# A never-taken, hinted branch at the end of TensorE's and VectorE's programs

## The chip, the cores, the metric

The kernel runs on one core of a Trainium2 chip. The metric is the device time of one execution in microseconds. A profiled execution also has a *span*, from its first to its last instruction. The time is a little longer than the span; below, time minus span of the same execution is called the **excess**. Spans of single runs are kept to 0.1 us, so a single excess is known to about 0.05 us. In the kernel before, the excess was 1.21 to 1.39 us in every run for which both are known. The engines go by the profiler's names: PE is TensorE, DVE is VectorE, ACT is ScalarE, POOL is GpSimd, and SP (SyncE) issues the output store and all loads but x's 2 KB, which ACT issues.

## The reference

One decode step: x plus grouped-query attention over a cache of 65,536 keys (4 KV heads, 32 query heads, head size 128), plus a small two-layer MLP branch, all in bf16.

```python
xn = _layernorm(x)
# A: q = xn @ wq; softmax(q k^T / sqrt(128)) v per head; @ wo
# B: x1 = xn + shift-mixed gelu(ln(xn) @ w1) @ w2;  x1 + gelu(ln(x1) @ w3) @ w4
return x + _A_ref(xn, k_cache, v_cache, wq, wo) + _B_ref(xn, w1, w2, w3, w4)
```

With one token there is almost no arithmetic per byte. The kernel's work is to read 170 MB of cache and weights once.

## The kernel before

The program records each engine's operations in a list (`q_pe`, `q_dve`, `q_act`, `q_pool`, `q_sp`), with semaphore waits worked out from the buffers, and then emits the lists one engine after another. All loads but x's go through SP's DMA queue; K and V arrive in 8 MB blocks, and the next block is issued when its slot is free. The main part, cut:

```python
for m in range(NBLK):                 # 8 blocks of 32768 keys, two per KV head
    ...
    Ttr(n); QK(n); ...                # DVE transposes K, PE multiplies
    MAX(..); EXP(..); PT(..); PV(..)  # softmax and P @ V
    issue(6 + 2 * m)                  # next loads
    ...
    if nb == BPH - 1:
        combine(h)
...
resid_rows()
wo_rows()
for i, (r0, nr) in enumerate(w4_parts):      # w4 comes in four pieces: 17, 7, 3, 1 rows
    out_rows([...], [b_W4[i], b_gh], last=...)
_op(q_dve, lambda e: e.tensor_copy(orow[:, :], OUT), ...)
ev_out = _dma(q_sp, chan("out"), lambda e: e.dma_start(out=..., in_=orow[0:97:32, :]), ...)
q_sp.wait_all([ev_out])                      # SP alone waits for the output
```

DVE's program is one straight line of about 270 instructions. PE's has a loop over the four heads, and after it the straight tail:

```python
q_dve.emit(nc.vector)
...
with nc.tensor.Fori(0, HKV):
    ...
q_pe.emit(nc.tensor, q_pe.ops[marks[-1]:])   # everything after the loop
```

## Time and profile before

| | before |
|---|---|
| median time of the first three runs | 400.42 us (400.32 to 400.59) |
| span of the profiled run | 399.1 us |
| bytes read | 169.87 MB, 426 GB/s over the span |
| instruction packets after the first instruction | five of 16,384 bytes, two of 8,192 bytes |

From the page of the kernel before: the line of the span; the rows of DMA share (each digit is a fortieth of the span, 9 means 90% or more) and GB/s; the DMA queues with packets, MB and the share of the 16 DMA engines' time; and the shares of the chain of waits.

```profile
span 399.1 us, 3429 instructions
...
DMA  9999899999999999999999999999999999999995
GB/s 420 420 388 493 383 441 466 447 415 427 420 427 429 434 460 434 434 427 420 434 427 420 466 440 434 421 420 434 427 427 466 434 440 420 420 427 434 418 414 229
...
q1 hardware_dynamic: 3608, 169.87, 98.7%
q8 instruction: 5, 0.08, 0.1%
q10 hardware_dynamic: 144, 0.00, 0.0%
q14 instruction: 2, 0.02, 0.0%
HBM read 169.87 MB, written 0.00 MB: 426 GB/s over the span
...
DMA 59%; DVE 25%; PE 12%; issue 1%; ACT 1%; SPq 1%; POOL 0%
```

DMA holds 59% of the chain that ended last. The two `instruction` queues, q8 and q14, bring program code. They take 0.1% of the engines' time, which seems too little to matter. The page counts two packets on q14 after the first instruction.

From the chain of waits of the kernel before, its end (start us, length us, what):

```profile
363.64 32.91 DMA KV<-in_B_w_dram
396.56 0.04 issue
396.60 0.31 PE S_ps L566 x4
396.91 0.02 issue
396.94 0.42 DVE orow L647
```

The last piece of w4 lands at 396.56 us; four matmuls and a copy follow. From the timeline, the output store:

```profile
397.39 0.63 SPq L648 DMA_DIRECT2D out_dram<-orow  x1
```

Its wait ends at 399.08 us, and with it the span. Now the same queues in two stretches: 255 to 262 us, and 392 to 396 us, where the last pieces of w4 arrive (DMA view restricted to a window).

```profile
DMA packets 59, 3.02 MB, mean 432 GB/s; under 512 B 12, under 2 KB 12, under 8 KB 12
...
q1 hardware_dynamic: 58, 3.01, 100.2%
q14 instruction: 1, 0.01, 0.3%
```

```profile
q1 hardware_dynamic: 283, 1.06, 65.7%
q8 instruction: 1, 0.02, 1.7%
```

Each stretch has one instruction packet among the data packets. The packet records give the times of all seven (start us from the span's start, length us, bytes):

```
q8   46.00  1.09  16384      q14   52.71  0.33  8192
q8   81.76  1.03  16384      q14  259.38  0.33  8192
q8  122.72  1.02  16384
q8  378.24  1.07  16384
q8  394.28  1.08  16384
```

The first two q8 packets fall 257 PE instructions apart (182 and 439 had started before them); the third comes 268 later, and the last two, both behind the loop, are 301 apart. Before the two q14 packets 51 and 190 DVE instructions had started.

```
241.76 .79 .82 .87 .88 .92 .98 242.03 .11 .27 .38 .39 | 242.90 243.35 243.53 243.71
261.12 .15 .18 .23 .24 .28 .35 .39 .47 .64 .75 .75   | 262.71 262.89 263.07 263.24
394.45 .48 .52 .56 .61 .66 .81 .88 .96 395.07 .08    | 396.02 396.11 396.20 396.39 396.56
```

Twelve engines form a pack. Four are late by 0.51, 0.96, 1.14 and 1.32 us after the pack's last one in the first row. In the second row, after the packet at 259.38 us, the engine with 0.51 is gone and one with 1.49 is there. In the last row the pack has lost one more engine, after the q8 packet at 378.24 us. The same comparison around q8's first three packets shows one engine of the pack 1.55 to 1.56 us later each time, so a 16 KB packet cost more than the "about 1 us" that the prediction below gives every fetch.

### The profile page before, as it was taken

What the parts mean: (1) busy time and instruction counts of PE and PEld (TensorE: products, weight loads), DVE (VectorE), ACT (ScalarE), POOL (GpSimd) and SP (SyncE); (2) the same over time, 40 slices, a digit from 0 to 9 for tenths busy, and PEclk for the clock granted to TensorE, in tenths of its full rate; (3) what the DMA queues carried; (4) which work ended last, traced back from release to release, by engine and by line L of the source; (5) the groups of instructions that cost most, each with busy time, mean ns of one, the idle gap of its engine ahead of it and who ended that gap; (6) DMA issues with size and microseconds to landing.
All of it is one profiled execution on the core that took longest, in us unless ns stands there. A gap on an engine that the chain in (4) does not pass through costs nothing.

```text
span 399.1 us, 3429 instructions
## 1 busy us (share of the span) xinstructions
PE 168.9 (42%) x1523; PEld 59.0 (15%) x1484; DVE 221.4 (55%) x260; ACT 23.9 (6%) x50; POOL 7.7 (2%) x31
## 2 busy tenths in 40 slices
PE   0034767338033713460357036413541362137394
PEld 0011334012001210110012001101120110012232
DVE  0024222994298549833984597269647952895201
ACT  1000000011001100110011002000100110011000
POOL 5000000000000000000000000000000000000000
PEclk9998568555655665575557555855585558555969
DMA  9999899999999999999999999999999999999995
GB/s 420 420 388 493 383 441 466 447 415 427 420 427 429 434 460 434 434 427 420 434 427 420 466 440 434 421 420 434 427 427 466 434 440 420 420 427 434 418 414 229
DMA packets 3759, 169.97 MB, mean 426 GB/s; under 512 B 548, under 2 KB 552, under 8 KB 808
## 3 DMA queue, kind: packets, MB, share of 16 engines
q1 hardware_dynamic: 3608, 169.87, 98.7%
q8 instruction: 5, 0.08, 0.1%
q10 hardware_dynamic: 144, 0.00, 0.0%
q14 instruction: 2, 0.02, 0.0%
HBM read 169.87 MB, written 0.00 MB: 426 GB/s over the span
## 4 chain that ended last, share of the span: by engine, by line
DMA 59%; DVE 25%; PE 12%; issue 1%; ACT 1%; SPq 1%; POOL 0%
DMA KV<-in_A_k_cache_dram 45%; DVE KV L460 18%; DMA KV<-in_B_w_dram 8%; DMA KV<-in_A_x_dram 6%; PE S_ps L411 3%; PE OT_ps L518 2%; DVE mrow L481 2%; PE M_ps L426 2%; PE S_ps L474 2%; PE S_ps L379 1%; ACT p_sb L496 1%; DVE Yall L395 1%; DVE pT_f L509 1%; DVE pT_f L419 1%; PE PT_ps L505 0%
## 5 line engine op out<-in xcount | busy, mean ns | idle before, releaser
L460 DVE STREAM_TRANSPOSE KV<-KV 128x4096 f32<-128x4096 f32 x32 | 140.3, 4422 | 44.3 <-DMA KV<-in_A_k_cache_dram 44.3
L474 PE MATMUL S_ps<-KV,Ycur 128*32 128x512 bf16 x512 | 60.7, 624 | 132.5 <-DVE KV L460 132.5
L518 PE MATMUL OT_ps<-KV,pT_f 128*32 128x512 bf16 x512 | 47.2, 511 | 4.0 <-issue 3.0
L474 PEld LDWEIGHTS S_ps<-KV,Ycur 128*32 128x32 bf16 x512 | 14.3, 126 | 160.0 <-DVE KV L460 142.4
L496 ACT ACTIVATE p_sb<-S_ps,brun 128x1024 bf16<-128x1024 f32 x16 | 17.8, 1114 | 276.6 <-DVE brun L494 176.1
L509 DVE STREAM_TRANSPOSE pT_f<-PT_ps 128x512 f32<-128x512 f32 x32 | 22.5, 702 | 14.0 <-PE PT_ps L505 14.0
L481 DVE TENSOR_REDUCE mrow<-S_ps 128x1 f32<-128x1024 f32 x16 | 19.3, 1205 | 11.3 <-PE S_ps L474 11.3
L484 PE MATMUL M_ps<-Rm,Lmat 128*128 128x16 bf16 x16 | 3.1, 194 | 38.0 <-DVE Rm L482 38.0
L529 DVE SCALAR_TENSOR_TENSOR O_acc<-O_acc,ff,OT_ps 128x512 f32<-128x512 f32 x12 | 9.0, 748 | 14.7 <-PE OT_ps L518 14.7
L518 PEld LDWEIGHTS OT_ps<-KV,pT_f 128*32 128x32 bf16 x512 | 13.1, 115 | 23.8 <-issue 16.4
L411 PE MATMUL S_ps<-KV 128*32 128x512 bf16 x88 | 12.1, 538 | 2.7 <-DVE KV L359 2.7
L339 DVE CAST KV<-KV 128x8 f32<-128x8 bf16 x1 | 0.2, 172 | 22.2 <-DMA KV<-in_A_x_dram 22.2
L578 PE MATMUL S_ps<-KV,o_bf 128*1 128x512 bf16 x64 | 9.9, 484 | 4.5 <-DMA KV<-in_A_wo_dram 4.5
L505 PE MATMUL PT_ps<-p_sb,permR 128*128 128x512 bf16 x16 | 9.7, 607 | 0.8
L426 PE MATMUL M_ps<-ident_f,pT_f 64*128 64x2 f32 (+2 forms) x32 | 7.9, 373 | 2.5 <-DVE pT_f L419 2.5
L484 PEld LDWEIGHTS M_ps<-Rm,Lmat 128*128 128x128 bf16 x16 | 1.7, 104 | 49.3 <-DVE Rm L482 49.3
L582 DVE COPY pT_f<-S_ps 1x512 f32<-1x512 f32 x1 | 0.7, 679 | 14.4 <-PE S_ps L578 14.4
L426 PEld LDWEIGHTS M_ps<-ident_f,pT_f 64*128 64x128 f32 (+2 forms) x32 | 7.7, 326 | 4.7 <-DVE pT_f L419 3.1
L419 DVE COPY pT_f<-S_ps 64x512 f32<-64x512 f32 (+1 forms) x3 | 2.1, 685 | 10.8 <-PE S_ps L411 10.8
L505 PEld LDWEIGHTS PT_ps<-p_sb,permR 128*128 128x128 bf16 x32 | 3.3, 102 | 27.5 <-ACT p_sb L496 14.7
L364 PE MATMUL M_ps<-KV 8*128 8x8 bf16 x1 | 0.2, 184 | 16.1 <-DVE Dmat_f L363 16.1
L642 POOL MEMSET pT_f<- 64x512 f32 x1 | 0.5, 520 | 312.4 <-PE OT_ps L518 312.4
(88 smaller groups left out, 90.2 us busy)
## 6 DMA issues: line engine op xcount, KB each, us to landing
KV<-in_B_w_dram SPq DMA_DIRECT2D x1, 7168.0 KB, 48.0
KV<-in_B_w_dram SPq DMA_DIRECT2D x1, 4352.0 KB, 27.4
KV<-in_B_w_dram SPq DMA_DIRECT2D x2, 2048.0 KB, 28.3
KV<-in_B_w_dram SPq DMA_DIRECT2D x1, 1792.0 KB, 31.3
KV<-in_B_w_dram SPq DMA_DIRECT2D x1, 768.0 KB, 32.7
KV<-in_B_w_dram SPq DMA_DIRECT2D x1, 256.0 KB, 32.9
KV<-in_A_k_cache_dram SPq DMA_DIRECT2D x8, 46.7
KV<-in_A_v_cache_dram SPq DMA_DIRECT2D x8, 28.1
```

The source lines that it names most:

```text
L411: fns.append(lambda e, j=j, k=k, mv=mv: e.matmul(S_ps[32 * (k % 4):32 * (k % 4) + 32, bank + k // 4, :], vec[:, j:j + 1].broadcast_to([P, ...
L419: _op(q_dve, lambda e, b=b, nb=nb: e.tensor_copy(pT_f[0:32 * nb, b, :], S_ps[0:32 * nb, bank + b, :]), reads=[b_S[bank + b]], writes=[b_pT ...
L426: fns.append(lambda e, b=b, nb=nb, c=c: e.matmul(M_ps[:, c0 + 16 * b + c:c0 + 16 * b + 4 * nb:4], pT_f[0:32 * nb, b, c:512:4], ident_f[0:3 ...
L460: _op(q_dve, lambda e: e.transpose(out=KV32[:, s, o:o + 4096], in_=KV32[:, s, o:o + 4096]), reads=[b_KV[s][sub]], writes=[b_KV[s][sub]], l ...
L474: fns.append(lambda e, we=we, cm=cm, mv=mv: e.matmul(S_ps[32 * cm:32 * cm + 32, n % 4, :], Ycur[:, we, :, :].rearrange("p a g -> p (a g)") ...
L481: _op(q_dve, lambda e: e.reduce_max(mrow[:, k:k + 1], S_ps[:, 2 * k:2 * k + 2, :].rearrange("p b c -> p (b c)"), axis=AX.X), reads=b_S[2 * ...
L496: _op(q_act, lambda e: e.activation(p_sb[:, :, :].rearrange("p b c -> p (b c)"), S_ps[:, 2 * k:2 * k + 2, :].rearrange("p b c -> p (b c)") ...
L505: _op(q_pe, lambda e: e.matmul(PT_ps[:, :], permR[:, :], p_sb[:, n % 2, :], start=True, stop=True), reads=[b_p[n % 2], b_const], writes=[b ...
L509: _op(q_dve, lambda e: e.transpose(out=pT_f[:, n % 2, :], in_=PT_ps[:, :]), reads=[b_PT], writes=[b_pT[n % 2]], loop=True)
L518: fns.append(lambda e, q=q, q4=q4: e.matmul(OT_ps[32 * q4:32 * q4 + 32, g % 2, :], pT_bf[:, n % 2, q, :, 1], KV[:, s, 8192 * sub + 512 * q ...
L529: _op(q_dve, lambda e: e.scalar_tensor_tensor(out=O_acc[:, 0:512], in0=O_acc[:, 0:512], scalar=ff[:, k:k + 1], in1=OT_ps[:, k, :], op0=ALU ...
L578: _grp(q_pe, [lambda e, j=j, jj=jj: e.matmul(S_ps[32 * jj:32 * jj + 1, 1, :], o_bf[:, j:j + 1], KV[:, 0, j * D + 512 * jj:j * D + 512 * (j ...
```

## The change

The intent: an instruction packet for code that never runs in the kernel costs DMA time for nothing. So the last block of code on PE and DVE starts with a branch hint (the trace lists it as BRANCH_PREFETCH_HINT, in the profiled run of the change at 142.49 us on DVE and 391.07 us on PE, 0.05 us each) and ends with the branch that the hint is tied to in the program, which is never taken. The intent is to keep away the packets that come last; whether a hint does that is for the runs to show.

```diff
             if nb == BPH - 1:
                 combine(h)
+            if m == 1:
+                dve_cut = len(q_dve.ops)
 ...
         wo_rows()
+        pe_cut = len(q_pe.ops)
 ...
-        q_dve.emit(nc.vector)
+        def hinted_tail(eng, ops, at, name):
+            q, e = ops, eng.engine
+            never = eng.alloc_register(name + "_r")
+            eng.reg_mov(never, 1)
+            nc.br(name + "_b", engines=[e])
+            label(name + "_t")
+            eng.nop(nofuse=True)
+            nc.br(name + "_end", engines=[e])
+            label(name + "_b")
+            hint = eng.mark_branch_hint_location()
+            q.emit(eng, q.ops[at:])
+            eng.wait_ge(ev_out[0], ev_out[1])
+            eng.br_eq(never, 0, on_true=name + "_t", on_false=name + "_end").branch_hint(hint)
+            label(name + "_end")
+        q_dve.emit(nc.vector, q_dve.ops[:dve_cut])
+        hinted_tail(nc.vector, q_dve, dve_cut, "dve")
 ...
-        q_pe.emit(nc.tensor, q_pe.ops[marks[-1]:])
+        q_pe.emit(nc.tensor, q_pe.ops[marks[-1]:pe_cut])
+        hinted_tail(nc.tensor, q_pe, pe_cut, "pe")
 ...
```

One line is cut here: the code is now in several blocks, and the pass that drops repeated weight loads is pointed at the right one; the count of weight loads stays 1484. PE and DVE now wait for the output before they leave, which only SP did before.

## The prediction

> **What bounds the kernel.** The DMA stream does. The page's slice rows show DMA at 9 tenths or more in 39 of 40 slices at about 427 GB/s; 169.87 MB are read in 399.1 us. The chain of waits gives DMA 59% of the span, DVE 25%. DVE is 55% busy, PE 42%. The last load (the last row of w4) lands at 396.56 us, and only 2.5 us follow it.

> **What the change touches.** Instruction fetches. [...] the DMA part of the page lists two instruction queues, and the packet records put five 16,384-byte packets on q8 (at 46.0, 81.8, 122.7, 378.2 and 394.3 us; 1.02 to 1.09 us each[...]) and two packets of 8,192 bytes, half that size, on q14 (52.7 and 259.4 us; 0.33 us each), which I read as DVE's. The last of each, 394.3 and 259.4 us, should be the useless ones[...].

> **What they cost.** The 16 completion increments of each load show the 16 DMA engines one by one. Before the first fetch they lie within 0.6 us; from then on each fetch puts one engine about 1 us behind for good[...]. The 259.4 us fetch moves one engine from 0.52 to 1.5 us behind the pack. That engine becomes the last to land, but only 0.17 to 0.18 us after the next laggard, which other fetches, that stay, have made late. So without it the last load should land at about 396.39 instead of 396.56 us: 0.17 us gained. The 394.3 us fetch came when its engine was nearly done with the last load: between the last two w4 pieces all sixteen increments moved by 0.64 to 0.65 us except two, by 0.72 and 0.74, both early ones. Its removal gains nothing.

> **What it adds.** PE and DVE each get a register move, two branches, a nop (jumped over), a hint, a wait on the output and the closing compare-branch. The trace has 29 ns for a move and 76 ns for an untaken compare-branch (207 to 226 taken). The front part runs while both engines wait for DMA, so it costs nothing. The closing branch runs after the output landed: about 0.1 us at the end, which takes back half of the gain.

> **Prediction.** 400.3 us, range 399.9 to 400.7; faster by over 2%: 0.5%, within 2%: 98.5%, slower: 1%.

> **What would show each step right or wrong.** q14 should have one packet inside the kernel instead of two, q8 four instead of five. The landings after 260 us should have four laggards at most 1.32 us behind the pack, until the 378 us fetch adds a fifth. The last w4 landing moves by 0.1 to 0.25 us. Last instructions should be PE's or DVE's branch, not SP's wait.

> **What would make it wrong.** [...] A block not prefetched may have to be fetched on demand when the engines run on past the kernel's end, after the output[...]. [...]

The forecast's sum: 0.17 us gained in the span, half of it taken back by about 0.1 us at the end, from 400.42 us, gives the 400.3 us. That the last packet of each queue is useless stands as the author's estimate. The runs bear it out: e4 did without both and gave correct results. "About 1 us" for each fetch is rough: by the increments above it was 0.98 us at 8 KB and 1.55 to 1.56 us at 16 KB, and at the packet of 394.28 us no increment moved against the others by more than 0.1 us.

## The result

| | before | after |
|---|---|---|
| median of six runs | 400.50 us (400.32 to 400.77) | 400.87 us (400.58 to 401.81) |
| span of the profiled run | 399.1 us | 398.8 us |
| last load landed, profiled run | 396.56 us | 396.23 us |
| excess | 1.23 us in the profiled run | 1.48 to 2.71 us, mean 2.02 |

The ratio of the runs is 1.0013, 95% interval 1.0000 to 1.0026. A ratio here is the mean time of one kernel's runs over that of the other's of the same rounds, so it is not quite the ratio of the medians. The median went up while the span of the profiled run went down, and the median lies 0.17 us above the range of the prediction.

The same lines of the page after:

```profile
span 398.8 us, 3437 instructions
...
DMA  9999999999999999999999999999999999999995
...
q1 hardware_dynamic: 3608, 169.87, 98.8%
q8 instruction: 4, 0.07, 0.1%
q10 hardware_dynamic: 144, 0.00, 0.0%
q14 instruction: 2, 0.02, 0.0%
...
DMA 59%; DVE 25%; PE 13%; issue 1%; ACT 1%; SPq 1%; POOL 0%
```

q8 has lost one packet, as predicted. q14 still counts two, which was not. The end of the chain and the output store:

```profile
363.30 32.93 DMA KV<-in_B_w_dram
396.23 0.04 issue
396.28 0.31 PE S_ps L566 x4
396.58 0.02 issue
396.61 0.42 DVE orow L650
```

```profile
397.06 0.63 SPq L651 DMA_DIRECT2D out_dram<-orow  x1
```

Everything from the last landing to the store is as before, only 0.33 us earlier. The front part cost nothing, as predicted, although only DVE was waiting for DMA: DVE ran it from 142.2 to 142.5 us and then stood idle until 146.76 us for a K load; PE ran it from 390.7 to 391.1 us among its matmuls, whose groups L584 and L566 start 0.54 us apart as before (390.73 and 391.27 us, before 390.83 and 391.37). The last instruction is now PE's closing branch, as predicted: SP's wait ends at 398.74 us, 0.34 us earlier than before, and the branch, 0.08 us long, ends the span at 398.82 us. In the stretch of 255 to 262 us:

```profile
DMA packets 61, 3.15 MB, mean 449 GB/s; under 512 B 13, under 2 KB 13, under 8 KB 13
...
q1 hardware_dynamic: 61, 3.15, 103.9%
```

The packet is gone. In 392 to 396 us:

```profile
q1 hardware_dynamic: 290, 1.08, 67.1%
q14 instruction: 1, 0.01, 0.5%
```

PE's packet is gone, but an 8 KB packet on q14 (at 394.00 us by the records) has come in. The increments of the three loads after the change:

```
241.77 .79 .85 .91 .93 .94 .96 .97 242.31 .35 .46 .49 | 243.01 243.51 243.51 243.53
261.13 .16 .23 .26 .30 .30 .32 .35 .68 .70 .82 .85   | 262.37 262.88 262.88 262.89
394.49 .50 .61 .63 .65 .66 395.01 .04 .15 .18 .31    | 395.68 396.18 396.19 396.22 396.23
```

The step between the first two rows is gone: the late engines are 0.52, 1.02 to 1.03 (two) and 1.04 us behind in both. So DVE's packet is gone with its delay, as predicted. What is left to explain is the excess.

### The profile page after: what moved, and what is told of

It is laid out like the page before. It is cut to its first block, busy times and chain, and to the rows that moved or that the text cites. A ratio compares the mean times of both kernels' runs of the same rounds, so it can differ in the third digit from the quotient of the medians.

```text
span 398.8 us, 3437 instructions
## 1 busy us (share of the span) xinstructions
PE 170.4 (43%) x1523; PEld 59.5 (15%) x1484; DVE 221.4 (56%) x260; ACT 23.9 (6%) x50; POOL 7.6 (2%) x31
## 3 DMA queue, kind: packets, MB, share of 16 engines
q1 hardware_dynamic: 3608, 169.87, 98.8%
HBM read 169.87 MB, written 0.00 MB: 426 GB/s over the span
## 4 chain that ended last, share of the span: by engine, by line
DMA 59%; DVE 25%; PE 13%; issue 1%; ACT 1%; SPq 1%; POOL 0%
DMA KV<-in_A_k_cache_dram 45%; DVE KV L460 18%; DMA KV<-in_B_w_dram 8%; DMA KV<-in_A_x_dram 6%; PE S_ps L411 3%; PE OT_ps L518 2%; DVE mrow L481 2%; PE M_ps L426 2%; PE S_ps L474 2%; PE S_ps L379 1%; ACT p_sb L496 1%; DVE Yall L395 1%; DVE pT_f L509 1%; DVE pT_f L419 1%; PE PT_ps L505 0%
```

## The experiments

Two theories were stated first. **A**: what the hint keeps out of the kernel is fetched when the engine runs on past the kernel's code, after the output has landed: outside the span, inside the time. **B**: the closing waits and branches themselves make the end longer. The kernels of one group ran on one chip, beside runs of the kernel before. Judged by time alone, most of them cannot be told from the kernel before: only the intervals of e8 to e10, e12 and e14 exclude a ratio of 1. So the excess and the traces carry the argument; in the kernel before the excess stays within 0.18 us.

### First group: parts of the change (e1 to e4)

**e1**, the hinted tail on DVE alone (`q_pe.emit(nc.tensor, q_pe.ops[marks[-1]:])` as before):

> Hinted tail on DVE alone. Theory A (a fetch that the hint keeps out of the kernel is made on demand after the output has landed, outside the span but inside the time): the 8 KB fetch near 259 us is gone and the q8 fetch near 394 us is back; last landing near 396.2 to 396.4, span 398.7 to 399.1. If DVE's own code block runs out after the kernel, the time stays 1.5 us or more above the span and the median is 400.6 to 401; if only PE pays, the excess is back at 1.25 us and the median 400.1 to 400.3. Theory B (the closing waits and branches themselves delay the end): about half of the change's excess, 0.2 us above the kernel before whatever was fetched.

**e2**, on PE alone (`q_dve.emit(nc.vector)` as before):

> Hinted tail on PE alone. Theory A: the q8 fetch near 394 us is gone, the q14 fetch near 259 us is back, last landing 396.5 as before, span 399.1 to 399.2; the time is 400.5 if PE has room left in its last block for what runs after the kernel, and 400.8 to 402 if PE pays on demand. Theory B: about 0.2 us above the kernel before.

**e3**, both tails without the hint:

```diff
-            hint = eng.mark_branch_hint_location()
-            eng.br_eq(...).branch_hint(hint)
+            eng.br_eq(...)
```

> Both tails with their jumps, waits and closing branches, but without the two hint instructions. Theory A: both fetches are back (q14 near 259, q8 near 394), last landing near 396.5, span 399.1 to 399.2, excess of time over span 1.25 us, median 400.5 to 400.6, tight. Theory B: fetches are back too, but the time stays near 400.9 or more with a spread of over 1 us, since waits and branches are all there.

**e4**, the change without the wait for the output:

```diff
-            eng.wait_ge(ev_out[0], ev_out[1])
```

> As the change, but PE and DVE do not wait for the output before their closing branch. Theory A: the fetches inside stay away, last landing 396.2 to 396.4; PE and DVE run past their branches at about 396.7 and 397.1, so that a fetch on demand is under way while the output is stored (2 us): excess over the span back to 1.2 to 1.4 us, median 400.0 to 400.3, tight. If the fetch takes longer than the store, part of the excess stays. Theory B (the wait is the cost) expects the same fall here, but then e3 must stay slow.

The 2 us that e4's expectation gives the store is an estimate; in the profiled run of the kernel before 1.69 us pass from the store's issue at 397.39 us to the end of SP's wait at 399.08 us.

Measured, five runs each, against nine of the kernel before (mean span 399.27 us, mean excess 1.26, median time 400.56):

| | median time | mean span | excess: mean (all) | packet at 259 | q8 packet at 394 |
|---|---|---|---|---|---|
| e1 DVE alone | 400.43 | 399.06 | 1.38 (1.32 to 1.50) | gone | there |
| e2 PE alone | 400.97 | 399.22 | 1.76 (1.52 to 2.30) | there | gone |
| e3 no hint | 400.76 | 399.18 | 1.58 (1.55 to 1.62) | there | there |
| e4 no wait | 400.27 | 399.00 | 1.32 (1.27 to 1.40) | gone | gone |

The hint is what removes packets: without it (e3) both are back. The span falls where DVE's packet is gone and hardly moves where PE's is. The excess is a matter of PE: it stays low with DVE's tail alone, though e1's median of 400.43 us is above the 400.1 to 400.3 that A gave. Both theories have a part: e3, with no hint at all, keeps an excess of 1.58 us, which A did not expect; but it is tight, while the hinted PE of e2 scatters up to 2.30, which B did not expect.

### Second group: the wait, the best version, the change again, a doubled fetch (e5 to e8)

**e5** is e3 without the wait; **e6** is e1 without the wait; **e7** is the change once more.

> Both tails as bare jumps and closing branches: no hint, no wait for the output. Known so far: time minus span is 1.26 us in the kernel before, 1.57 with both tails unhinted but waiting (e3), 1.3 hinted without the wait (e4). If that 0.3 us of e3 is the closing wait, the excess is back at 1.25 to 1.35 here, both fetches (259 and 394 us) are back, last landing about 396.5, span 399.1 to 399.3, time 400.4 to 400.6. If it is the branches that cost, the excess stays at 1.5 or more.

> Hinted tail on DVE alone, without the wait for the output. Theory A: keeps the whole gain (no fetch at 259 us) and pays nothing at the end: last landing 396.2 to 396.5, excess 1.25 us, time 400.2 to 400.4, faster than the kernel before by 0.1 to 0.3 us. Rival (the gain of e4 came from PE's missing fetch at 394): time as the kernel before, 400.5.

> The change itself once more, on the chip of e5 and e6. Theory A: span 0.1 to 0.4 us under the kernel before, excess of time over span 1.5 to 2.7 us and scattered, median 400.7 to 401.2. Rival (the slower times were that chip's or that set's noise): excess 1.3, time at or under the kernel before.

Five runs of each. Before on this chip, nine runs: mean span 399.14, mean excess 1.27, median 400.41.

| | median time | mean span | excess: mean (all) |
|---|---|---|---|
| e5 no hint, no wait | 400.56 | 399.26 | 1.27 (1.22 to 1.33) |
| e6 DVE alone, no wait | 400.35 | 399.06 | 1.26 (1.23 to 1.28) |
| e7 the change | 400.68 | 399.04 | 1.76 (1.48 to 2.25) |

e5 against e3: the 0.3 us goes with the wait, not with the branches. e7 repeats the result: a shorter span, a longer and scattered excess. e6 keeps its excess at 1.26 us; its time is 0.06 us under the kernel before by medians, ratio 0.9998 (0.9984 to 1.0011), so not clear of noise.

**e8** was to double the suspected cost inside: the kernel before with 256 waits that are already met (two come in one instruction: its page has 3557 instructions against 3429, so 128 more), for one more code packet for DVE; q14 has three on its page.

```diff
+        for k in range(256):
+            q_dve.ops.append((0, chans["x"].sem, 16))
         for m in range(NBLK):
```

> The kernel before with 128 more instructions on DVE (waits that are already met), in a stretch where DVE waits 30 us for the first K load, so that DVE crosses one more block boundary: a doubled suspected cost. If every DVE fetch sets the same DMA engine back by about 1 us for good, there are three fetches on q14 (52, about 75 to 85, 259 us), one engine ends about 2.3 to 2.6 us behind the pack instead of 1.5, last landing about 397.4 to 397.7, span and time about 1 us longer (401.2 to 401.7). If a fetch's delay is absorbed, or lands on another engine each time, the last landing stays within 0.3 us of 396.5.

It failed as an experiment: 408.91 us. DVE was not idle there: the first K block lands at 69.5 us in the kernel before and its transposes start at once. The 128 instructions took 12.7 us (DVE's idle time in the timeline between 70.5 and 83.2 us), the first block was late, and DMA ran dry, as the page's DMA row shows in the 11th fortieth:

```profile
DMA  9999999999299999999999999999999999999995
```

Nothing about a fetch's cost can be read from its time, except that one such padding instruction takes about 0.1 us on DVE. Its increments do show one: with the added q14 packet at 87.58 us, one engine goes from 1.32 us behind the first one (the load complete at 69.4 us) to 2.36 us behind (the load complete at 89.1 us), by about 1 us.

### Third group: behind the branch, PE's wait alone, the doubled fetch done properly (e9 to e12)

**e9** lets PE run 200 more instructions after its hinted branch, so that what follows it lies inside the trace; **e10** is the same without the hint.

```diff
         hinted_tail(nc.tensor, q_pe, pe_cut, "pe")     # without the wait for the output
+        for k in range(400):
+            nc.tensor.wait_ge(chans["x"].sem, 16)      # already met, two per instruction
```

> PE alone has the hinted tail, without the wait for the output, and after its closing branch runs 200 more instructions (waits already met) past the end of the code block, so that what happens behind the branch falls inside the trace. Theory A (the hint suppresses the fetch, and the block is fetched when it is needed): no q8 fetch at 394 us; a q8 fetch of 16 KB starts only after the closing branch (397 us or later), and in PE's run of waits there is one gap[...]. If the gap is there, an on-demand fetch is shown with its length; if the fetch starts right behind the branch and no gap is seen, the block is only fetched later. Rival (the hint does no more than move the fetch or skip a useless one): no q8 fetch after 394 and no gap.

> The control of the run before: the same 200 instructions, no hint. The q8 fetch near 394 us is there, no gap over 0.3 us in PE's run of waits; perhaps one more q8 fetch as PE crosses into the next block. PE's run ends[...] earlier than with the hint if theory A holds, at the same time if not.

The DMA queues in e10 (no hint), 392 to 397 us and then 397 to 400 us; PE's closing branch is at 397.01 us:

```profile
q1 hardware_dynamic: 283, 1.05, 52.9%
q8 instruction: 1, 0.02, 1.4%
```

```profile
q1 hardware_dynamic: 8, 0.00, 0.3%
```

And in e9 (hint), the same two stretches; PE's branch is at 397.13 us:

```profile
q1 hardware_dynamic: 289, 1.11, 54.9%
q14 instruction: 1, 0.01, 0.4%
```

```profile
q8 instruction: 1, 0.02, 2.8%
q1 hardware_dynamic: 8, 0.00, 0.3%
```

Without the hint the code packet comes at 394.02 us, among the loads. With it, it comes at 398.17 us, 1.04 us after the start of the branch and 0.96 us after its end. So where code follows, the hint does not save the fetch: in this pair of traces it **postpones** it until after the branch. The gap that A expected in PE's run of waits is missing, with no idle stretch over 0.22 us: the trace does not show PE waiting for the packet, and its run ends 0.38 us later than in e10. The next q8 packets come at 410.46 us here and 409.67 in e10. The times were 420.56 and 420.27 us (two runs each); both are long because of the 200 added instructions. Their excess, 1.49 to 1.53 us, is that of e11 below, although PE ends about 20 us after SP here: that PE is late seems to be enough; it need not meet SP.

**e11**: the kernel before plus one instruction, PE's wait for the output at its end.

```diff
         q_pe.emit(nc.tensor, q_pe.ops[marks[-1]:])
+        nc.tensor.wait_ge(ev_out[0], ev_out[1])
```

> The kernel before with one instruction more: PE waits for the output at its end. No branch, no hint, all fetches as before. If a PE that reaches the kernel's end together with SP is what lengthens the end, the excess of time over span is 1.5 to 1.6 us as in e3 (1.27 in the kernel before), span 399.1 to 399.3, median 400.6 to 400.8. If the branches are needed for the cost, excess 1.27 and time 400.4 to 400.5.

Measured: mean span 399.20 (before 399.21), excess 1.50 to 1.55, mean 1.53 (before 1.30), median 400.70 us (before 400.50). One wait is enough for 0.23 us in the excess.

**e12**: the doubled fetch, with the 128 instructions split over two stretches in which DVE waits 8 us for a K load.

```diff
             if nb == BPH - 1:
                 combine(h)
+            if m in (0, 2):
+                q_dve.ops += [(0, chans["x"].sem, 16)] * 128
```

> The doubled fetch again, with the 128 padding instructions (64 issued slots each, about 0.1 us apiece as e8 showed) split over two waits of DVE of 8 us, at 100 and 178 us, where they should delay nothing. Three fetches on q14 (about 53, 115 to 190, 259 us). If each sets the same DMA engine back 0.5 to 1 us for good: last landing 397.0 to 397.6 instead of 396.5, span and time 0.5 to 1.1 us longer than the kernel before. If fetches land on engines in turn or the delay is absorbed: last landing and time within 0.2 us of the kernel before.

From its page, the instruction queues, and from its chain of waits, the end:

```profile
q8 instruction: 5, 0.08, 0.1%
q10 hardware_dynamic: 144, 0.00, 0.0%
q14 instruction: 3, 0.02, 0.0%
```

```profile
364.75 32.91 DMA KV<-in_B_w_dram
397.65 0.04 issue
397.70 0.31 PE S_ps L566 x4
```

q14 has three packets (55.3, 143.3 and 258.1 us by the records), and the last load lands at 397.65 us. The median is 401.41 us, ratio 1.0022 (1.0009 to 1.0036); the mean span is 400.16 against 399.21. The increments show the engine going back step by step. Here are the late engines only, in us after the last one of the pack:

```
load landed at 126 us:   0.84  1.25  1.36  1.43
  (fetch at 143.3)
load landed at 165 us:   1.26  1.36  1.42  1.82      0.84 has become 1.82
load landed at 242 us:   1.27  1.37  1.43  1.83
  (fetch at 258.1)
load landed at 262 us:   1.24  1.36  1.41  2.79      1.83 has become 2.79
```

Two fetches of 8 KB moved the same engine by 0.98 and 0.96 us, for good. The cost of a code fetch in a stream that keeps DMA at 9 in 38 of the 40 slices, as e12's page shows, is thus measured. The packet itself takes only 0.33 us; why the delay is three times as long is open.

All the other traces agree. In each of the eight whose DVE has no hint (before, e2, e3, e5, e9, e10, e11, e17) one engine falls back by 0.96 to 0.98 us between the loads around 242 and 262 us; in the nine with DVE hinted (after, e1, e4, e6, e7, e13 to e16) none moves by more than 0.02 us. What this costs at the end differs, though: in those eight the engine that fell back is then 0.03 to 0.86 us behind the next one, depending on how far back it and the others stood before (it stood 0.47 to 0.99 us behind the pack).

### Fourth group: the order of branch and wait, and the owner of the new packet (e13, e14)

**e13**: the change with the wait moved behind the branch.

```diff
-            eng.wait_ge(ev_out[0], ev_out[1])
             eng.br_eq(never, 0, ...).branch_hint(hint)
             label(name + "_end")
+            eng.wait_ge(ev_out[0], ev_out[1])
```

> The change with one instruction moved: PE and DVE take their closing branch first and wait for the output after it. e9 showed that PE's postponed fetch starts 1 us after the branch. If the scattered part of the change's excess (1.5 to 2.7 us against 1.55 of a plain late PE, e3 and e11) is that fetch running past the output, it now runs under the store: excess 1.5 to 1.6 us and tight, span 0.1 to 0.3 under the kernel before, time 400.4 to 400.7. If the scatter comes from something else about a hinted end, it stays 1.5 to 2.7.

**e14**: e6, and ACT waits for the output at its end (`nc.scalar.wait_ge(ev_out[0], ev_out[1])` after `q_act.emit(nc.scalar)`).

> DVE's hinted tail without its wait, as e6, and ACT waits for the output at its end. In all hinted runs the unforeseen 8 KB fetch on q14 came 3.3 to 3.45 us after ACT's last instruction. If ACT makes it when it runs past the kernel's code, there is no q14 packet between 390 and 399 us here (it moves past the end of the trace); if it is DVE's, it stays at 393 to 394. Excess 1.3 to 1.4, time 400.2 to 400.5.

Five runs of e13 and four of e14. Before on this chip, nine runs: mean span 399.16, mean excess 1.30, median 400.47.

| | median time | mean span | excess: mean (all) |
|---|---|---|---|
| e13 | 400.60 | 399.04 | 1.55 (1.47 to 1.64) |
| e14 | 401.19 | 398.95 | 2.26 (2.23 to 2.32) |

e13 came out as expected in the numbers: the excess of all five runs is that of a plain late PE, without the scatter. Its trace does not show the expected reason, though: no q8 packet lies between PE's branch and the output, nor behind it within the records, and the trace of e4, whose PE also branches before the output has landed, has none either.

e14 answered its question and showed more than was asked. The q14 packet at 393 to 394 us is gone, so it was ACT's; it now stands behind the output. From the DMA view of e14, 399 to 402 us, after the span's end at 398.7 us:

```profile
DMA packets 1, 0.01 MB, mean 3 GB/s; under 512 B 0, under 2 KB 0, under 8 KB 0
...
q14 instruction: 1, 0.01, 0.6%
```

By the records it starts at 400.34 us, 1.6 us after ACT's last instruction; the time of that execution was 401.02 us. The excess is 2.26 us in the mean, 0.96 more than before, and my expectation of 1.3 to 1.4 was wrong. This is what theory A describes, but on ACT: an engine that arrives late and still fetches goes with a time longer by almost 1 us, and no span shows it. How much of the 0.96 us is the fetch and how much ACT's late arrival alone (PE's cost 0.23 us in e11, without such a fetch) was not separated: no run has ACT wait in a kernel without a hint, where no such packet of ACT was seen.

### Last group: a trace of the scatter (e15 to e17)

Unaltered kernels, one look each: the change (e15, e16) and PE's tail alone (e17, the kernel of e2).

> The change once more, for its trace: about one run in four of a hinted PE that waits had an excess over 2.2 us, and no such run has a trace yet. If a trace with an excess over 2 us is caught and holds an instruction packet behind the output, the scatter is a fetch on demand; if it holds none, it is not, and it stays open. A trace with an excess of 1.5 to 1.8 us tells nothing new.

> The same as e15, for a second chance at a trace with an excess over 2 us: a packet on q8 or q14 behind the output if the scatter is a fetch, none if it is not.

> PE's hinted tail alone (the kernel of e2) for a trace: excess 1.5 to 2.3 us; if it is over 2 us, a q8 packet behind the output if the scatter is a fetch, none if it is not.

The excesses were 1.82, 1.54 and 1.67 us, so no run over 2 us was caught. From 399.4 us, behind the span's end at 399.3 us, e15's queues show

```profile
DMA packets 1, 0.02 MB, mean 6 GB/s; under 512 B 0, under 2 KB 0, under 8 KB 0
...
q8 instruction: 1, 0.02, 2.2%
```

and e16's, behind its end at 399.2 us, show

```profile
DMA packets 0, 0.00 MB, mean 0 GB/s; under 512 B 0, under 2 KB 0, under 8 KB 0
```

e17 has none either. e15's packet starts at 400.48 us, 1.15 us after the end of PE's branch; in e9 it was 0.96 us. So PE's postponed fetch can occur behind the output in the change. It was recorded in one of the four traces of the change only: the first one has nearly the same excess (1.81 us) and no such packet. And e15's packet lasts until 401.41 us by the records, although the time of that execution was 401.12 us. Where that time starts against the span's zero is not recorded; unless it starts 0.29 us or more after the first instruction, this execution was over before the packet was, and its excess is no wait for it.

## Why the prediction was wrong

**Right: what bounds the kernel, and which packets go.** DVE's packet at 259 us and PE's at 394 us disappear, and the hint does it (e3). That the packets go with the engines' own instructions is shown as far as this: the first two q8 packets are 257 PE instructions apart and the next comes 268 later, 128 more DVE instructions brought one more packet on q14 (e12), and each hint removed a packet on one queue (q14's with DVE's in e1, q8's with PE's in e2). How an engine decides when to fetch was not shown.

**Right: the mechanism of the cost inside; its size in part by luck.** 0.17 us was predicted from the late engines of one trace. That one engine would no longer fall back by about 1 us holds in every trace. But the gain is only what that engine was behind the next one, and in the eight traces without DVE's hint this is 0.03 to 0.86 us: that the one at hand had 0.17 us, close to the average found, is luck. Over the six kernels with DVE hinted that have a kernel before on the same chip (e1, e4, e6, e7, e13, e14) the mean span is 0.08 to 0.27 us under the kernel before, 0.16 on average; with DVE unhinted and the rest of the kernel as before (e2, e3, e5, e11) it is between 0.09 under and 0.12 over, 0.01 under on average. (In e1, e2, e3 and e7 the span includes a closing branch of 0.07 to 0.08 us after the output.) e12 shows the mechanism by doubling it. That PE's packet at 394 us costs nothing in the span agrees with e2 (0.05 under). The 0.33 us between the first two traces is not a measure of it: in the four traces of the change the last load landed at 396.23, 396.57, 396.64 and 396.75 us. Over all traces it landed at 396.50 us on average in the nine with DVE hinted and at 396.71 us in the eight without.

**Wrong: the end.** The step that failed is "about 0.1 us at the end, which takes back half of the gain". It counted the closing branch (73 and 83 ns after the output, as the trace has it), which was right and lies inside the span, and left out what a late PE does to the time behind the span. There the excess grew by 0.49 us (e7 against its kernel before), and in the first six runs it was 2.02 us against 1.23 us in the profiled run before. The runs showed two terms in its place:

1. PE arriving at the end only after the output costs 0.23 us (e11, no branch at all); both engines late cost 0.32 us (e3). DVE's share is small: e1's excess is 0.12 over before. This is shown. Why PE's late arrival costs more than DVE's is not.
2. A hinted PE whose branch comes after the wait has a further, scattered cost: excess 1.48 to 2.71 us over all runs of the change, 1.52 to 2.30 in e2, against 1.50 to 1.62 for an unhinted late PE (e3, e11) and 1.47 to 1.64 when the branch comes first (e13). That the hint and the order decide is shown, for the order by five runs. A postponed fetch of PE is shown in e9 and, behind the output, in e15; that a late engine with a fetch behind the end goes with 0.96 us is shown for ACT (e14), late arrival and fetch together. That the scatter *is* PE's fetch is not shown, and its cause stays open: no run with an excess over 2 us has a trace, one trace with 1.81 has no packet, and the packet of e15 seems to outlast the execution.

The sum for e7, on its chip: −0.10 us in the span, +0.49 us in the excess. The prediction did name a fetch on demand behind the output as what would make it wrong, but its range of 399.9 to 400.7, which ends 0.28 us above the 400.42 us of the kernel before, gave that almost no room, and the wait for the output on PE was read as free.

**Wrong: the packet count on q14.** One was predicted inside the kernel; there were two. The new one comes in each recorded hinted kernel, 3.0 to 3.5 us after ACT's last instruction, and in none without a hint; e14 shows that it is ACT's. Landing among the last loads, it did no harm that the spans show. Why a hint on PE or DVE makes ACT fetch is open.

**A version that beats both?** e4 (no wait) and e6 (DVE alone, no wait) keep the gain inside and avoid the loss at the end: medians 400.27 against 400.56, and 400.35 against 400.41. Their ratios, 0.9996 and 0.9998, are not clear of noise. If this change is worth having, it is on DVE alone and without the wait, since the packet of PE cost nothing that the spans show; its size is about 0.16 us of 400.

## What to carry to other kernels

Where the page shows DMA as busy as here (9 in 38 of 40 slices), look at the 16 increments of a load one by one: here a code packet of 8 KB set one of them back by 0.96 to 0.98 us for good, and one more such packet made the kernel 0.91 us longer (e12: 401.41 against 400.50 us). Such a delay costs only what that increment is behind the next one at the last load, here 0.03 to 0.86 us. How far it is then behind the next one differs from run to run, so read it from more than one trace. When work is moved past the last instruction, compare time and span: the span can shrink while the time grows (e7: the span 0.10 us less, the excess 0.49 us more). An engine that is made to wait for the output arrives late at the end; here that cost 0.12 us for DVE, 0.23 us for PE and, with a fetch behind the end, 0.96 us for ACT.
